# First additions held in their written order on VectorE, and a first norm in larger portions

## The chip, the cores and the metric

The kernel runs on one core of a Trainium2 chip. The metric is the device time of one execution in microseconds (us), as the median of several runs. A core has engines that run their own instruction streams side by side: TensorE (PE) does matmuls into PSUM, VectorE (DVE) and ScalarE (ACT) do element-wise work, GpSimd (POOL) helps in the first half, and SyncE (SP) issues the DMA transfers. Engines wait for each other through semaphores.

## The reference

Three blocks follow each other on 8 sequences of 576 tokens with 512 channels:

```python
# attention: 8 heads of 64, mask by blocks of 64 tokens
attn = softmax(where(block_i >= block_j, q @ k.T / 8, -1e9)) ; x = attn @ v
# gated mixer
gate = sigmoid(causal_conv(x, conv_w))            # 5 taps, by channel
x = (gate * (x @ w_val)) @ w_out
# Fourier mix, norm and feed-forward
u  = x + real(fft(fft(x, axis=1), axis=2))
un = (u - mean(u)) / sqrt(var(u) + 1e-6)
out = u + relu(un @ w_ch1) @ w_ch2                # 512 -> 2048 -> 512
```

## The kernel before

Products of fp32 numbers are made as three matmuls of high and low parts: every operand x is split into h (a cast on ScalarE) and x - h (a subtraction on VectorE).

The first 640 us are attention, mixer and transform; they write u, tokens along the free axis, to the tensor u_d. The rest is the norm and the feed-forward, and only that is touched.

**Straight products.** The first two blocks of 512 tokens (g = 0 and 1) go through the 16 blocks f of the weights with plain products: psh (lines 1489 to 1491), its relu split into HL (h on ScalarE, line 1493, low part on VectorE, line 1494), and the second product into o (1509 to 1511), one block behind. Beside them weights are loaded, decoded and summed (`combine`: four additions on VectorE at line 1203, a cast on ScalarE at 1227, low part at 1228, store to comb_d). In g = 1, from f = 6, the norm of the first pair of blocks is made beside them, by calls of `next(nxt)`, some steps at each f.

**Pairs.** The remaining tokens go in four pairs (blocks of 512, 512, 384 and 384 tokens) through products with seven in place of eight partial products. A pair has 56 steps n: in the first 28 (l = 0) four rounds i over the seven partial products in the order 1, 2, 6, 5, 7, 3, 4; in the last 28 (l = 1) seven over four i. A step is 12 matmuls into a pair of PSUM banks (`product`, lines 1414 to 1416). The banks are read out by a copy on ScalarE (1422) or an addition on VectorE (1427); 1424 is an addition of h to h, 1430 and 1432 are the relu. Partial product 6 of a round adds to the sums of partial product 1, two steps after it, and needs the copy of 1422 first. `prepare(k + LOOK)` makes an operand three steps ahead: ScalarE's cast at 1374, VectorE's low part at 1375, its source at 1319 (a difference of blocks). The operands lie in a ring of eight places, `ring_o = [10, 11, 12, 13, 8, 9, "HH", "U1"]`; the last one is also the source of the stores out<-U (line 1525) of the second straight block.

Three generators run beside the steps. `combine2` makes the other weight sums in units of a weight block: four additions on VectorE (`four`, line 1203), four casts packed<-two on ScalarE (1257), four low parts (1260), four stores to comb_d of 256 KB (1246). The packed buffers are two each of KP and KL, so the casts of one unit wait until the stores of the unit before have landed. `norm_x(g + 1)` makes the norm of the next pair, from X (loaded from u_d by `load_x` at n = 0): the sums u2 + u3 (line 1118, the first addition), u0 + u1 (1119) and their sum (1120), split into ah (1108, ScalarE) and al (1109, VectorE) for the mean on TensorE (1111, 1112); then X minus mean (1128), squares (1133), their sums (1135), root (1140), reciprocal (1141) and the scaling of X (1312). `load_chunk` loads weights; `load_y` loads u for the residual.

A scheduler orders the instructions of each engine by its own costs and the order in which the program traces them; `tc.keep_in_program_order(x)` ties an instruction behind all that was traced on its engine before it. SP's queue carries all transfers.

Of the kernel before, what the change touches and what calls it, by code (L numbers as in the profile page):

```python
# [9 lines left out]
F32R = mybir.dt.float32r  # L10
# [7 lines left out]
def kernel(  # L18
# [1030 lines left out]
    def phase2():  # L1049
        with ExitStack() as c2:  # L1050
# [61 lines left out]
                nc.tensor.matmul(ps, ones, l, start=False, stop=True)  # L1112
                yield

            def norm(u, n, done, hl=None, first=False):
                pool = nc.vector
                s1, s = (s2.tile([P, T], F32, tag="x", name=x)[:, 0:n] for x in ("s1", "s"))
                nc.vector.tensor_tensor(out=s1, in0=u[:, 2, :], in1=u[:, 3, :], op=ALU.add)
                pool.tensor_tensor(out=s, in0=u[:, 0, :], in1=u[:, 1, :], op=ALU.add)
                nc.vector.tensor_tensor(out=s, in0=s, in1=s1, op=ALU.add)  # L1120
                yield
                pm = ps_t.tile([P, T], F32, tag="t", name="pm")[:, 0:n]
                yield from average(pm, s, n, first)
                q = s5.tile([P, T], F32, tag="s", name="q")[:, 0:n]
                for t in range(4):
                    x = s2.tile([P, T], F32, tag="x", name="x")[:, 0:n]
                    c = x if hl else u[:, t, :]
                    nc.vector.tensor_tensor(out=c, in0=u[:, t, :], in1=pm, op=ALU.subtract)
                    if hl:
                        nc.scalar.copy(out=hl[0][:, t, :], in_=x)  # L1130
                        (pool if t % 2 else nc.vector).tensor_tensor(
                            out=hl[1][:, t, :], in0=x, in1=hl[0][:, t, :].bitcast(F32), op=ALU.subtract)
                    nc.scalar.activation(out=x if t else q, in_=c, func=AF.Square)
                    if t:
                        pool.tensor_tensor(out=q, in0=q, in1=x, op=ALU.add)
                    yield
                pv = ps_t.tile([P, T], F32, tag="t", name="pv")[:, 0:n]
                yield from average(pv, q, n, first)
                r = s5.tile([P, T], F32, tag="r", name="r")[:, 0:n]
                nc.scalar.activation(out=r, in_=pv, func=AF.Sqrt, bias=eps)  # L1140
                nc.vector.reciprocal(out=r, in_=r)
                yield
                yield from done(r)
# [43 lines left out]
            def load_w(f):  # L1187
# [9 lines left out]
                nc.scalar.copy(out=h, in_=x)  # L1197
                nc.vector.tensor_tensor(out=l, in0=x, in1=h.bitcast(F32), op=ALU.subtract)

            def four(t, a11, a12, a21, a22):  # L1200
                for z, a, b, op in ((0, a21, a22, ALU.add), (1, t[:, 0], a11, ALU.subtract),
                                    (2, a11, a21, ALU.subtract), (3, a12, t[:, 1], ALU.subtract)):
                    nc.vector.tensor_tensor(out=t[:, z], in0=a, in1=b, op=op)

            def combine():

# [27 lines left out]
            def combine2():  # L1234

                ins = {}

                def load(j):
                    if j < NH:
                        ins[j] = [kp.tile([P, S], F32, tag=t, name="ab")[:, 0:D] for t in ("K0", "K1")]  # L1240
                        for z in range(2):
                            nc.sync.dma_start(out=ins[j][z], in_=w_d[j + NH * z][:, D:2 * D])
                def keep(j, p):
                    z, jj = divmod(j, NH // 2)
                    for s in range(4):
                        nc.sync.dma_start(out=comb_d[1][z][s][:, jj * D:jj * D + D], in_=p[s].bitcast(F32))
                load(N2A)
                for j in range(N2A, NH):
                    load(j + 1)
                    yield  # L1250
                    x = [x.rearrange("p (y c) -> p y c", c=256) for x in ins.pop(j)]
                    t = s3.tile([P, 4, 256], F32, tag="st", name="two")
                    p = [kp.tile([P, S], F32R, tag=n, name="packed")[:, 0:D] for n in ("KP", "KL", "KP", "KL")]
                    four(t, x[0][:, 0], x[1][:, 0], x[0][:, 1], x[1][:, 1])
                    yield
                    for s in range(4):
                        nc.scalar.copy(out=p[s][:, 0:256], in_=t[:, s])
                    yield
                    for s in range(4):
                        nc.vector.tensor_tensor(out=p[s][:, 256:D], in0=t[:, s], in1=p[s][:, 0:256].bitcast(F32),  # L1260
                                                op=ALU.subtract)
                    yield
                    yield
                    keep(j, p)
# [41 lines left out]
            def norm_x(g):  # L1306
                if g >= NQ:
                    return
                for z in range(2):
                    def scale(r, u=X[g, z]):  # L1310
                        for t in range(4):
                            nc.vector.tensor_tensor(out=u[:, t, :], in0=u[:, t, :], in1=r, op=ALU.mult)
                            yield
                    yield from norm(X[g, z], NS[g], scale)

            T2 = {}

# [45 lines left out]
            def operand(k):  # L1363

                if k >= len(steps):
                    return
                g, l, p, i = steps[k]
                if l == 0 and i:
                    opnd[k] = opnd[k - 7]
                    return  # L1370
                x = source(k)
                o = at(ring_o[nitem[0] % len(ring_o)], [P, 2, 2, NS[g]], F32R, "o")
                nitem[0] += 1
                nc.scalar.copy(out=o[:, 0], in_=x)  # L1374
                nc.vector.tensor_tensor(out=o[:, 1], in0=x, in1=o[:, 0].bitcast(F32), op=ALU.subtract)  # L1375
                opnd[k] = o
# [84 lines left out]
            for g in range(NG):  # L1461
# [4 lines left out]
                for f in range(NF + 1):  # L1466
# [31 lines left out]
                        next(mix, None)  # L1498
                    if f > LG and late:
                        late.pop(0)()  # L1500
                    for _ in range(2 if g == 0 and f >= NL else 3 if g and f >= 6 else 1):
                        next(nxt, None)
                    if f == 0:
                        continue
# [30 lines left out]
            for k, (g, l, p, i) in enumerate(steps):  # L1535
                n = k % 56
                if n == 0:
                    load_x(g + 1)
                    nxt = norm_x(g + 1)
                if k % 2 == 0 and k:  # L1540
                    load_chunk(k // 2 + len(ring_w) - 1)
                if 24 <= n < 28:
                    load_y(g, (11, 12, 22, 21)[n - 24])
                prepare(k + LOOK)
                if n < 24:
                    next(mix, None)
                early(g, l, n - 28 * l)
                product(k)
                if n >= LP and late:
                    late.pop(0)()  # L1550
                if n >= 12:
                    next(nxt, None)

    phase1()
# [95 lines left out]
```

## Time and profile before

| what | us |
|---|---|
| median of 3 runs | 1416.41 |
| lowest and highest | 1414.26, 1420.87 |
| the profiled execution | 1415.93 |
| its span on the core | 1414.1 |
| TensorE busy in the span | 1353.9 (96%) |
| VectorE, ScalarE, GpSimd busy | 1097.1, 821.9, 207.8 |

A row of a timeline gives the start of an instruction from the span's start, how long it took, its engine and line, what it writes and reads (tile names without numbers), shape, and in square brackets how long the engine had been idle before it and what ended that. Equal neighbours are put into one row with a count. A matmul's record is longer than its share of TensorE, since matmuls are pipelined; the distance of two starts is what one costs. The granted clock (PEclk) is 1.00 or 0.50 of full speed.

### The profile page before, as it was taken

The page shows a single profiled execution, that of the slowest core. Times are in us where ns is not written, and L with a number is a line of the kernel's source. Part 1 is how long each engine was busy: PE and PEld are TensorE (multiplying, and loading weights), DVE is VectorE, ACT ScalarE, POOL GpSimd, SP SyncE. Part 2 cuts the span into 40 slices and gives each one's busy share as a digit, 9 for nine tenths or more (in the row PEclk, how much of TensorE's full clock was granted, in tenths as well). Part 3 has the DMA queues.
Part 4 walks back from the last instruction along what each step waited for, and adds up shares of the span by engine and source line. Part 5 has one row for each costly group of instructions (what it writes and reads, how often), then busy time and mean ns, then how long its engine had stood idle before and what let it go on. Part 6 is the DMA issues. An engine that isn't in the chain of part 4 may idle for free.

```text
span 1414.1 us, 24025 instructions
## 1 busy us (share of the span) xinstructions
PE 1353.9 (96%) x8547; PEld 1188.6 (84%) x8547; DVE 1097.1 (78%) x1965; ACT 821.9 (58%) x1790; POOL 207.8 (15%) x180
## 2 busy tenths in 40 slices
PE   5798999999999999999999998999999999999998
PEld 3576889898989898988787887788878889999998
DVE  5777697878878787989899798599637983796374
ACT  5677777687777777755344344564346533644451
POOL 3423232323232322321100000000000000000000
PEclk9799999999999999999999999999999999999999
DMA  7566666656565565546798976975875579779875
GB/s 211 147 174 191 154 177 162 179 140 182 142 176 153 159 159 147 168 141 226 249 331 317 369 281 213 322 237 197 283 254 201 179 244 321 251 251 323 271 249 188
DMA packets 176755, 308.24 MB, mean 218 GB/s; under 512 B 28270, under 2 KB 106876, under 8 KB 169468
## 3 DMA queue, kind: packets, MB, share of 16 engines
q1 hardware_dynamic: 176096, 306.57, 68.8%
q8 instruction: 68, 1.11, 0.3%
q14 instruction: 51, 0.42, 0.1%
q10 hardware_dynamic: 540, 0.14, 0.1%
HBM read 203.74 MB, written 56.76 MB: 184 GB/s over the span
## 4 chain that ended last, share of the span: by engine, by line
PE 70%; DVE 12%; DMA 7%; ACT 4%; issue 3%; POOL 2%; SPq 1%; DVEq 0%; ACTq 0%; POOLq 0%
PE banks L1414 11%; PE banks L1415 11%; PE banks L1416 11%; PE av L615 4%; PE pt L587 4%; PE sc L427 2%; DVE gate L642 2%; PE sc L428 2%; PE psh L1489 2%; PE psh L1491 2%; PE psh L1490 2%; PE o L1511 2%; PE o L1509 2%; PE o L1510 2%; PE psx L191 1%
## 5 line engine op out<-in xcount | busy, mean ns | idle before, releaser
L1414 PE MATMUL banks<-o,chunk 128*128 128x512 f32 (+1 forms) x896 | 326.3, 364 | 8.4 <-ACT h L1422 8.1
L1415 PE MATMUL banks<-o,chunk 128*128 128x512 f32 (+1 forms) x896 | 325.3, 363 | 0.0
L1416 PE MATMUL banks<-o,chunk 128*128 128x512 f32 (+1 forms) x896 | 325.3, 363 | 0.0
L473 ACT ACTIVATE PB<-sc,mx 128x128 f32<-128x128 f32 (+4 forms) x320 | 166.5, 525 | 51.5 <-DVE mx L459 27.8
L1414 PEld LDWEIGHTS banks<-o,chunk 128*128 128x128 f32 x896 | 168.9, 189 | 28.6 <-ACT h L1422 10.5
L1416 PEld LDWEIGHTS banks<-o,chunk 128*128 128x128 f32 x896 | 168.8, 188 | 17.8
L1415 PEld LDWEIGHTS banks<-o,chunk 128*128 128x128 f32 x896 | 169.0, 189 | 17.4
L1374 ACT CAST o<-h 128x1024 fp32r<-128x1024 f32 (+1 forms) x112 | 105.6, 945 | 112.2 <-PE banks L1416 93.9
L587 PE MATMUL pt<-ident,PB 128*128 128x128 f32 x800 | 141.4, 283 | 15.6 <-ACT PTb L593 8.1
L1375 DVE TENSOR_TENSOR o<-h,o 128x1024 fp32r<-128x1024 f32 (+1 forms) x112 | 119.7, 1088 | 28.0 <-ACT o L1374 20.9
L587 PEld LDWEIGHTS pt<-ident,PB 128*128 128x128 f32 x800 | 100.7, 144 | 32.3 <-ACT PTb L593 14.4
L642 DVE SCALAR_TENSOR_TENSOR gate<-XF,cw,gate 128x575 f32<-128x575 f32 (+3 forms) x128 | 122.5, 957 | 4.5 <-ACT gate L63 3.8
L459 DVE TENSOR_REDUCE mx<-sc 128x1 f32<-128x384 f32 (+2 forms) x192 | 104.3, 560 | 4.4 <-PE sc L193 2.7
L427 PE MATMUL sc<-K,QQ 128*128 128x256 f32 (+2 forms) x256 | 87.7, 353 | 12.9 <-DMA QQ<-QHL 12.0
L593 ACT COPY PTb<-pt 128x512 f32<-128x512 f32 (+1 forms) x160 | 86.5, 544 | 18.5 <-PE pt L587 17.8
L1422 ACT COPY h<-banks 128x1024 f32<-128x1024 f32 (+1 forms) x64 | 57.9, 906 | 53.0 <-PE banks L1416 52.8
L191 PE MATMUL psx<-GH,we_h 128*128 128x290 f32 x256 | 84.3, 329 | 2.4 <-ACT GH L57 1.5
L191 PE MATMUL psv<-XH,wv_h 128*128 128x288 f32 x256 | 83.4, 326 | 0.4 <-ACT PB L473 0.4
L428 PE MATMUL sc<-KL,QQ 128*128 128x256 f32 (+2 forms) x256 | 82.8, 334 | 0.0
L638 POOL TENSOR_TENSOR XL<-XF,XH 128x576 fp32r<-128x576 f32 x32 | 45.9, 1434 | 248.9 <-ACT XH L57 248.7
L1319 DVE TENSOR_TENSOR h<-h 128x1024 f32<-128x1024 f32 (+1 forms) x64 | 69.1, 1089 | 10.8 <-ACT h L1430 10.5
L192 PE MATMUL psx<-GL,we_h 128*128 128x290 f32 x256 | 76.9, 300 | 0.5 <-DVE GL L703 0.5
(266 smaller groups left out, 3162.9 us busy)
## 6 DMA issues: line engine op xcount, KB each, us to landing
chunk<-comb_d SPq DMA_DIRECT2D x64, 512.0 KB, 5.4
chunk<-comb_d SPq DMA_DIRECT2D x32, 1024.0 KB, 4.8
chunk<-base_d SPq DMA_DIRECT2D x48, 512.0 KB, 6.1
chunk<-base_d SPq DMA_DIRECT2D x24, 1024.0 KB, 5.7
K<-KP SPq DMA_DIRECT2D x128, 144.0 KB, 2.5
QQ<-QHL SPq DMA_DIRECT2D x128, 128.0 KB, 2.5
rw<-in_w_ch SPq DMA_DIRECT2D x28, 512.0 KB, 8.2
comb_d<-packed SPq DMA_DIRECT2D x12, 1024.0 KB, 9.3
```

The costliest lines, as they stand in the source:

```text
L191: nc.tensor.matmul(ps, lh, rh, start=first, stop=False)
L427: nc.tensor.matmul(t[:, o:o + w], q[:, 0, m], KK[p][h][:, 0:w], start=True, stop=False)
L428: nc.tensor.matmul(t[:, o:o + w], q[:, 1, m], KL[p][:, 0:w], start=False, stop=True)
L459: nc.vector.reduce_max(out=mx[:, j:j + 1], in_=t, axis=AX.X, negate=one)
L473: nc.scalar.activation(out=PB[i][:, k0:k0 + w], in_=t, func=AF.Exp, bias=nm, accum_out=su[:, at + j:at + j + 1])
L587: nc.tensor.transpose(ps[:, j, :], PB[i][:, (j0 + j) * P:(j0 + j + 1) * P], ident)
L642: nc.vector.scalar_tensor_tensor(out=gate[c][:, s:S], in0=XF[:, 0:S - s], scalar=cw[:, c, 4 - s:5 - s], in1=gate[c][:, s:S], op0=ALU.mult, ...
L1374: nc.scalar.copy(out=o[:, 0], in_=x)
L1375: nc.vector.tensor_tensor(out=o[:, 1], in0=x, in1=o[:, 0].bitcast(F32), op=ALU.subtract)
L1414: nc.tensor.matmul(to, wh, o[:, 0, x], start=first, stop=False, skip_group_check=not begin)
L1415: nc.tensor.matmul(to, wh, o[:, 1, x], start=False, stop=False, skip_group_check=not begin)
L1416: nc.tensor.matmul(to, wl, o[:, 0, x], start=False, stop=last, skip_group_check=not begin)
```

## The change

Five edits. (1) `norm` takes a flag `pin`: for the norms of the pairs after the first pair of blocks (g > 0), the first addition u2 + u3 is tied behind all that was traced on VectorE before it. (2) `four` does so with the first of its four additions, once `combine2` has begun. (3) The eighth operand of the ring (item 7) and all later ones count from place 0 of the ring again, so item 7 takes place 10, not U1. (4) In g = 1 from f = 6 on, the norm of the first pair is advanced by four steps at each f, before by three. (5) In the pair loop `combine2` is advanced at the steps 4 to 27, before at 0 to 23, and the next pair's norm from step 10, before from 12.

```diff
-            def norm(u, n, done, hl=None, first=False):
+            def norm(u, n, done, hl=None, first=False, pin=False):
...
-                nc.vector.tensor_tensor(out=s1, in0=u[:, 2, :], in1=u[:, 3, :], op=ALU.add)
+                add = nc.vector.tensor_tensor(out=s1, in0=u[:, 2, :], in1=u[:, 3, :], op=ALU.add)
+                if pin:
+                    tc.keep_in_program_order(add)
...
+            pin = [False]
+
             def four(t, a11, a12, a21, a22):
...
-                    nc.vector.tensor_tensor(out=t[:, z], in0=a, in1=b, op=op)
+                    made = nc.vector.tensor_tensor(out=t[:, z], in0=a, in1=b, op=op)
+                    if pin[0] and z == 0:
+                        tc.keep_in_program_order(made)
...
                     x = [x.rearrange("p (y c) -> p y c", c=256) for x in ins.pop(j)]
+                    pin[0] = True
...
-                    yield from norm(X[g, z], NS[g], scale)
+                    yield from norm(X[g, z], NS[g], scale, pin=g > 0)
...
-                o = at(ring_o[nitem[0] % len(ring_o)], [P, 2, 2, NS[g]], F32R, "o")
+                o = at(ring_o[nitem[0] if nitem[0] < 7 else (nitem[0] - 7) % len(ring_o)], [P, 2, 2, NS[g]], F32R, "o")
...
-                    for _ in range(2 if g == 0 and f >= NL else 3 if g and f >= 6 else 1):
+                    for _ in range(2 if g == 0 and f >= NL else 4 if g and f >= 6 else 1):
...
-                if n < 24:
+                if 4 <= n < 28:
                     next(mix, None)
...
-                if n >= 12:
+                if n >= 10:
                     next(nxt, None)
```

Each engine has as many instructions after as before; their order differs from the first pair's norm on. Seven lines come in ahead of the second half, so that lines move: 1118 stays, 1203 becomes 1207, 1257 becomes 1264, 1319, 1374, 1375, 1422, 1427 and 1494 become 1326, 1381, 1382, 1429, 1434 and 1501.

On VectorE, at the end of the second straight block, before (X_10248 and X_10245 are the first pair's two blocks, two and ab belong to the weight sums):

```order
L1494 SCALAR_TENSOR_TENSOR HL<-psh,HL 128x512
L1203 TENSOR_TENSOR two<-ab 128x256
L1109 TENSOR_TENSOR al<-q,ah 128x512
L1203 TENSOR_TENSOR two<-two,ab 128x256
L1203 TENSOR_TENSOR two<-ab,two 128x256
L1141 RECIPROCAL r<-r 128x512
L1228 TENSOR_TENSOR packed<-two,packed 128x4x256
L1312 TENSOR_TENSOR X_10248<-X_10248,r 128x512
L1494 SCALAR_TENSOR_TENSOR HL<-psh,HL 128x512
L1312 TENSOR_TENSOR X_10248<-X_10248,r 128x512 x3
L1494 SCALAR_TENSOR_TENSOR HL<-psh,HL 128x512
```

and after:

```order
L1143 RECIPROCAL r<-r 128x512
L1207 TENSOR_TENSOR two<-ab 128x256
L1319 TENSOR_TENSOR X_10248<-X_10248,r 128x512
L1207 TENSOR_TENSOR two<-two,ab 128x256
L1207 TENSOR_TENSOR two<-ab 128x256
L1207 TENSOR_TENSOR two<-ab,two 128x256
L1319 TENSOR_TENSOR X_10248<-X_10248,r 128x512 x3
L1234 TENSOR_TENSOR packed<-two,packed 128x4x256
L1501 SCALAR_TENSOR_TENSOR HL<-psh,HL 128x512 x2
```

The reciprocal has moved ahead of the low part that stood before it, and two low parts now follow each other behind the scaling.

On VectorE, some ten rows on, at the last operands of the first round, before:

```order
L1319 TENSOR_TENSOR X_10245<-T_10746,X_10245 128x1024
L1203 TENSOR_TENSOR two<-ab 128x256 x2
L1203 TENSOR_TENSOR two<-two,ab 128x256
L1319 TENSOR_TENSOR X_10245<-X_10245,T_10746 128x1024
L1375 TENSOR_TENSOR o<-X_10245,o 128x1024
```

and after:

```order
L1326 TENSOR_TENSOR X_10245<-T_10746,X_10245 128x1024
L1326 TENSOR_TENSOR X_10245<-X_10245,T_10746 128x1024
L1207 TENSOR_TENSOR two<-ab 128x256
L1382 TENSOR_TENSOR o<-X_10245,o 128x1024 x2
```

The two subtractions now follow each other, and one addition of the weight sums is left beside the operands.

On ScalarE, in the first two rounds of the first pair (banks_10768 to banks_10770 are the three pairs of PSUM banks), before:

```order
L1374 CAST o<-X_10245 128x1024
L1257 CAST packed<-two 128x256 x3
L1374 CAST o<-X_10245 128x1024
L1422 COPY h<-banks_10768 128x1024
L1257 CAST packed<-two 128x256
```

and after, there and some ten rows on:

```order
L1381 CAST o<-X_10245 128x1024 x2
L1429 COPY h<-banks_10768 128x1024
L1437 ACTIVATE h<-h 128x1024
...
L1429 COPY h<-banks_10769 128x1024
L1264 CAST packed<-two 128x256 x2
L1108 CAST ah<-s 128x512
L1264 CAST packed<-two 128x256
L1437 ACTIVATE h<-h 128x1024
L1429 COPY h<-banks_10769 128x1024
```

The packed casts have left the place ahead of the first round's copy and stand between two copies of the second round.

## Rows read from the trace of the kernel before

**Rows 1.** The page, part 1: busy time, share of the span and instructions.

```profile
PE 1353.9 (96%) x8547; PEld 1188.6 (84%) x8547; DVE 1097.1 (78%) x1965; ACT 821.9 (58%) x1790; POOL 207.8 (15%) x180
```

**Rows 2.** TensorE's waits, 850 to 1414 us: total, times, longest, in us.

```profile
PE banks L1414 <- ACT h L1422: 8.1, 5, 3.5
PE banks L1414 <- DVE o L1521: 0.3, 1, 0.3
```

**Rows 3.** Windows: length, busy of PE, PEld, DVE, ACT, POOL, PEclk, DMA, GB/s.

```profile
863.00:869.80 6.80, 5.56 (x13) 4.41 (x14) 6.80 (x15) 2.59 (x5) 0.00 (x0) 0.50 0.72 217
...
950.00:1000.00 50.00, 50.00 (x222) 41.43 (x221) 49.46 (x52) 20.14 (x21) 0.00 (x0) 1.00 0.60 209
```

**Rows 4.** Timeline of TensorE: the last matmul before the long wait, and the waits.

```profile
860.33 0.39 PE L1416 MATMUL banks<-o,chunk 128*128 128x512 f32 x1
864.24 0.80 PE L1414 MATMUL banks<-o,chunk 128*128 128x512 f32 x1 [3.52 <-ACT h L1422]
...
896.02 0.51 PE L1414 MATMUL banks<-o,chunk 128*128 128x512 f32 x1 [1.44 <-ACT h L1422]
...
913.70 0.50 PE L1414 MATMUL banks<-o,chunk 128*128 128x512 f32 x1 [0.54 <-ACT h L1422]
...
1030.89 0.50 PE L1414 MATMUL banks<-o,chunk 128*128 128x512 f32 x1 [1.22 <-ACT h L1422]
...
1187.92 0.45 PE L1414 MATMUL banks<-o,chunk 128*128 128x384 f32 x1 [1.37 <-ACT h L1422]
```

**Rows 5.** Timeline of ScalarE, 860 to 864 us.

```profile
860.01 1.05 ACT L1374 CAST o<-X 128x1024 fp32r<-128x1024 f32 x1 [4.75 <-DVE X L1319]
860.96 1.01 ACT L1257 CAST packed<-two 128x256 fp32r<-128x256 f32 x3
862.23 1.04 ACT L1374 CAST o<-X 128x1024 fp32r<-128x1024 f32 x1 [0.25 <-DVE X L1319]
863.18 1.00 ACT L1422 COPY h<-banks 128x1024 f32<-128x1024 f32 x1
```

**Rows 6.** Timeline of VectorE, the same stretch.

```profile
859.88 0.76 DVE L1203 TENSOR_TENSOR two<-ab 128x256 f32<-128x256 f32 x2
860.56 0.42 DVE L1203 TENSOR_TENSOR two<-two,ab 128x256 f32<-128x256 f32 x1
860.89 1.23 DVE L1319 TENSOR_TENSOR X<-X,T 128x1024 f32<-128x1024 f32 x1
```

**Rows 7.** Timeline of VectorE, about the first pair's reciprocal.

```profile
839.63 0.69 DVE L1494 SCALAR_TENSOR_TENSOR HL<-psh,HL 128x512 fp32r<-128x512 f32 x1
...
842.74 3.35 DVE L1141 RECIPROCAL r<-r 128x512 f32<-128x512 f32 x1 [0.69 <-ACT r L1140]
```

**Rows 8.** Timeline of ScalarE, the operand cast before the wait at 896.

```profile
893.41 1.05 ACT L1374 CAST o<-h 128x1024 fp32r<-128x1024 f32 x1 [3.21 <-DMA chunk<-comb_d]
```

**Rows 9.** SP's queue, the last store of the second straight block.

```profile
884.63 0.40 SPq L1525 DMA_DIRECT2D out<-U  x1
```

**Rows 10.** Timeline of ScalarE, before the wait at 913.

```profile
910.90 0.88 ACT L1257 CAST packed<-two 128x256 fp32r<-128x256 f32 x2 [0.85 <-DMA comb_d<-packed]
```

**Rows 11.** Stores of a unit of weight sums on SP, ScalarE's casts behind them.

```profile
873.96 1.42 SPq L1246 DMA_DIRECT2D comb_d<-packed  x3
...
880.65 0.41 ACT L1257 CAST packed<-two 128x256 fp32r<-128x256 f32 x1 [0.38 <-DMA comb_d<-packed]
881.90 0.41 ACT L1257 CAST packed<-two 128x256 fp32r<-128x256 f32 x1 [0.84 <-DMA comb_d<-packed]
```

**Rows 12.** DMA issues: out<-in, queue, count, KB each, median us from issue to landing.

```profile
chunk<-comb_d SPq DMA_DIRECT2D x64, 512.0 KB, 5.4
...
comb_d<-packed SPq DMA_DIRECT2D x16, 256.0 KB, 7.6
```

**Rows 13.** Timeline of VectorE, the first additions of two later norms.

```profile
1026.27 0.56 DVE L1118 TENSOR_TENSOR s<-X 128x384 f32<-128x384 f32 x1 [6.15 <-DMA X<-u_d]
...
1184.26 0.56 DVE L1118 TENSOR_TENSOR s<-X 128x384 f32<-128x384 f32 x1 [4.97 <-DMA X<-u_d]
```

## The prediction, made before the changed kernel ran

> **What bounds the kernel now.** I read the page first: TensorE has a matmul running for 96% of the span [rows 1], so time can go only where it stands still or runs at its lower clock. Both kernels hold the same instructions and the order on the engines is the same up to about 803 us, so I asked for TensorE's waits from 850 us on, where the paired products begin. The reader is to see two entries: five waits of 8.1 us in all for line 1422, ScalarE's copy of a bank out of PSUM, and one of 0.3 us [rows 2]. Elsewhere TensorE is full: from 950 to 1000 us it is busy for 50.00 of 50 us with 222 matmuls [rows 3], that is one every 0.225 us, and VectorE beside it is busy for 49.46 us.
>
> A wait costs more than its idle time. A matmul's record lasts 0.39 us while the next begins after 0.225, so 0.16 us of the gap is already inside the record, and the first one behind a wait takes 0.50 us in place of 0.39 [rows 4]: together some 0.27 us on top. The five waits are then 1.44 + 0.27 = 1.7, 0.54 + 0.27 = 0.8, 1.22 + 0.27 = 1.5, 1.37 + 0.27 = 1.6 us, and the long one at 864.24. This one idles for 3.52 us and ends 864.24 - 860.33 - 0.225 = 3.7 us late. Behind it the granted clock is 0.50, which is 1.2 GHz, from 863.00 to 869.80 [rows 3]: 13 matmuls are busy for 5.56 us there, and at the full rate 13 take 2.9, so 2.6 us are lost besides. All five with the lower clock hold 11.9 us; no more can be had there.
>
> **The change part by part.** The sum is made against the profiled run, 1415.93 us with a span of 1414.1.
>
> *Late at the first pair (864.24).* The copy at 863.18 stands on ScalarE behind a cast of line 1374 that waited for VectorE [rows 5], and between them lie three packed casts of line 1257. VectorE had put three first-half additions of the later weight sums (line 1203, 859.88 to 860.97) ahead of the operand's subtraction at 860.89 [rows 6], and ran without a break. In the changed order the subtraction stands ahead of all but one of them and the packed casts have left ScalarE's row. On the other side, the larger portions bring the norm's reciprocal, 3.35 us, ahead of two low parts of line 1494, of which one was made at 839.63, before it [rows 7]. Walking VectorE's new row with the durations of the old one, TensorE misses that low part for about 1.65 us in the last straight products (between nothing and the reciprocal's 3.35), the operands of the first pair are done at 860.0 in place of 862.1, and the copy lets the product start at about 862.15 in place of 864.24: -2.1 us. The 1.65 us are not added, since the product that waited needs the copy, not TensorE's arrival; they use up the idle time that stood there. What is left of a wait there is some 0.2 us. Behind the waits of 1.22 to 1.44 us the first matmul takes 0.50 or 0.51 us, behind the long one 0.80 [rows 4]: the short ones brought no lower clock, so I take it as gone: -2.6 us. Moved with the norm are its two TensorE matmuls per sum, earlier by about two weight blocks and of the same number: nothing.
>
> *The operand ring (896.02).* ScalarE's cast of line 1374 at 893.41 idled for 3.21 us [rows 8]. The trace names a chunk load; the place it writes, U1, is also read by the store out<-U issued at 884.63 [rows 9], and 893.41 lies 8.8 us behind it, while that chunk has nothing to do with the place. Two bank copies stood behind it. In the new ring the cast takes place 10, and ScalarE's new order has it later, where no copy is due: -1.7. Every later operand moves on by one place; its last reader is then seven operands back, with 3 us or more of lead by my walk, at no cost. Without that lead each late operand would cost a step of 2.7 us.
>
> *Later weight sums four steps on.* A step is 12 matmuls, 12 x 0.225 = 2.7 us, so 16 stores, their 16 x 0.25 MB and the loads of ab leave SP's queue some 11 us later, and pass chunk and y loads on SP. This takes the wait at 913.70 away, where packed casts waited 0.85 us for a store [rows 10]: -0.8. It also makes a **new wait**. A unit's casts need the buffers that the unit before is still storing: in the kernel before, stores issued from 873.96 on let casts go at 880.65 and 881.90 [rows 11], 6.7 to 8.0 us later. In the new order the first unit's stores leave at about 875.5 to 876.3, and two packed casts of the second unit stand right behind the first copy of the second round, at which ScalarE arrives at 879.6. They wait until 882.2 to 884.3. Queued behind them on ScalarE are the norm's first cast, one more packed cast, a relu that wants a VectorE addition, and the bank copy that TensorE needs at 886.65 (862.15 and nine steps). By the walk that copy ends between 886.4 and 889.3, so this wait costs 0 to 2.9 us with the 0.27; I take 1.7, nearer to the upper landing since the median store takes 7.6 us [rows 12]: +1.7. The units after it have about 0.5 us in hand. The last chunk made of these sums stands behind the y loads on SP, and by a landing of 5.4 us [rows 12] still has some 5 us.
>
> The Trainium skill ("DMA: Bandwidth & Descriptors", section "Anatomy of one DMA — SWDGE (gpsimd) path") fits a DMA as about 2.0 us plus bytes over 436 GB/s, which would be an estimate of 2.6 us for such a store, and there would then be no new wait at all: the 1.7 us would drop out of the sum. The fit is for transfers that GpSimd issues, these are SP's, and the trace disagrees with it for them (6.7 us at the least).
>
> *First additions of the pairs' norms (1030.89, 1187.92).* VectorE sat on line 1118 for 6.15 and 4.97 us until the load of X landed [rows 13], with the addition or subtraction behind it that feeds ScalarE and so the copy. In the new order the addition stands behind the readouts of its step: -1.5 and -1.6. What is late next there is nothing on TensorE: the norm is used some 25 steps on. The start of the norm two steps earlier (n >= 10) can give back at most what these two removed, if the load is still not there.
>
> Sum: -2.1 - 2.6 - 1.7 - 0.8 - 1.5 - 1.6 + 1.7 = -8.6, so 1415.93 - 8.6 = 1407.3. The median of the runs before, 1416.41, is 0.5 above the profiled run, so on that scale **1407.8 us**. Faster or slower is called from 0.5% on (7.1 us, about what can be told from no change): faster means below 1409.3.
>
> **The rivals.** *No new wait:* stores land in 6 us or less. For it: two of the 16 need only be a little quicker. Against it: [rows 11, 12]. The sum is -10.3: 1406.1. *A long new wait:* the second unit's casts wait for the slower landing (2.9 us in place of 1.7) and TensorE falls to 1.2 GHz behind it as it did at 864.24, 2.6 more. That is -10.3 + 5.5 = -4.8: 1411.6. *The gain at the first pair does not come:* the missed low part costs the whole 3.35 us, the products start as late as before and the clock falls all the same. Left are -1.7 - 0.8 - 3.1 + 1.7 = -3.9: 1412.5. *Slower:* the stores of the later sums, now issued beside the round's chunk loads and out<-U stores, land after 11.5 us. ScalarE is then held for 5.8 us with the bank copy behind it and the lower clock after it (5.8 + 2.6), and the last chunk, behind the y loads, is 3.5 us late with the same (3.5 + 2.6): -10.3 + 14.5 = +4.2, 1420.6. It decides from landings above 11 us; the median of 7.6 speaks against it. *The change does not do what it says* (the tied additions stand where they stood): the orders shown above exclude it on VectorE.
>
> **How the numbers follow.** The forecast 0.42, no new wait 0.18, a long one 0.20, no gain at the first pair 0.12, slower 0.08. Faster holds "no new wait" and about 0.37 of the forecast (its upper end, 2.9 us of new wait, is 1409.0, and the runs spread): 0.55. The two long cases and the rest of the forecast are the same: 0.37. Slower: 0.08. The range goes down to all five waits gone, 1416.41 - 11.9 = 1404.5, and up beyond 1412.5 by half a microsecond: 1404.5 to 1413.0; the slower case and a part of the two long ones stay outside.
>
> **What would show it.** Right: no wait of over 0.5 us on the first pair's third product and a granted clock of 1.00 from 860 to 870; nothing near 1030 and 1187; a wait of 1 to 3 us of TensorE for the bank copy in the pair's second round, with ScalarE's packed cast idle for a store ahead of it. Wrong: a stall above 2 us in the last straight products, a stretch of 0.50 clock, a cast of an operand waiting for its ring place, or a new wait for a chunk at the end of the first pair.

## The result, and the profile after

The changed kernel takes 1406.13 us (median of 6 runs, 1404.02 to 1407.26), the kernel before 1417.37 (median of 6, 1414.26 to 1420.87): ratio 0.9919, 95% interval 0.9901 to 0.9937. The forecast was 1407.8 in a range of 1404.5 to 1413.0, and faster. The profiled runs are nearer to each other than the medians: 1415.93 before, low among its runs, and 1406.78 after, from the upper half of its own.

The page of the changed kernel answers [rows 1] with a span 9.1 us shorter:

```profile
span 1405.0 us, 24014 instructions
...
PE 1349.6 (96%) x8547; PEld 1186.2 (84%) x8547; DVE 1094.1 (78%) x1965; ACT 821.1 (58%) x1790; POOL 207.7 (15%) x180
```

Its TensorE waits from 840 us on, total, times and longest (before: [rows 2]): the five waits for the bank copy of line 1422, now 1429, have become one, and a wait for HL is new.

```profile
PE o L1518 <- DVE HL L1501: 1.7, 1, 1.7
PE banks L1421 <- ACT h L1429: 1.0, 1, 1.0
```

The two profiled runs already differ by some 0.6 us when the part with the change begins. For the comparisons I therefore take a stretch that both have: from the matmul that waits for the first decoded weights, just past 703 us, to the last matmul. Of the kernel before, TensorE's timeline has

```profile
703.13 0.50 PE L1489 MATMUL psh<-UTH,W 128*128 128x512 f32 x1 [1.09 <-ACT W L1197]
...
1409.76 0.34 PE L1416 MATMUL banks<-o,chunk 128*128 128x384 f32 x1
```

and of the changed one

```profile
703.76 0.50 PE L1496 MATMUL psh<-UTH,W 128*128 128x512 f32 x1 [1.02 <-ACT W L1199]
...
1400.60 0.34 PE L1423 MATMUL banks<-o,chunk 128*128 128x384 f32 x1
```

That is 706.63 and 696.84 us: 9.8 us less. I call it the **late stretch** below; it leaves out what goes on before 703.

At the start of the first pair, VectorE's timeline has the reciprocal 4 us earlier than in [rows 7], two low parts behind the scaling in one row, and the second subtraction at 859.09, not 860.89 [rows 6]:

```profile
838.72 3.35 DVE L1143 RECIPROCAL r<-r 128x512 f32<-128x512 f32 x1
...
846.96 1.28 DVE L1501 SCALAR_TENSOR_TENSOR HL<-psh,HL 128x512 fp32r<-128x512 f32 x2
...
859.09 1.22 DVE L1326 TENSOR_TENSOR X<-X,T 128x1024 f32<-128x1024 f32 x1
```

ScalarE's casts and the bank copy follow it, with no packed cast between them (before: [rows 5]):

```profile
860.42 1.06 ACT L1381 CAST o<-X 128x1024 fp32r<-128x1024 f32 x1 [0.16 <-DVE X L1326]
861.38 1.00 ACT L1429 COPY h<-banks 128x1024 f32<-128x1024 f32 x1
```

TensorE's timeline has the three places of which the prediction spoke, the wait for HL, the third product of the pair, and the new wait in the second round (before: [rows 4]):

```profile
847.70 1.21 PE L1518 MATMUL o<-HL,W 128*128 128x512 f32 x4 [1.67 <-DVE HL L1501]
...
862.43 0.50 PE L1421 MATMUL banks<-o,chunk 128*128 128x512 f32 x1
...
888.20 0.50 PE L1421 MATMUL banks<-o,chunk 128*128 128x512 f32 x1 [1.00 <-ACT h L1429]
```

The third product starts 0.28 us behind the matmul ahead of it (862.15), against 3.9 before, and the window from 863 on, with the columns of [rows 3], is at the full clock of 2.4 GHz:

```profile
863.00:870.00 7.00, 7.00 (x32) 5.81 (x31) 3.45 (x5) 2.97 (x3) 0.00 (x0) 1.00 0.87 281
```

The new wait is read on ScalarE and on SP. The casts behind the copy at 879.08 idle for a store. The relu behind them waits for an addition of VectorE (884.94 to 886.16), which stands behind the low parts of those casts, and the copy that TensorE needs ends at 888.15:

```profile
879.08 1.02 ACT L1429 COPY h<-banks 128x1024 f32<-128x1024 f32 x1 [1.43 <-PE banks L1423]
882.48 0.41 ACT L1264 CAST packed<-two 128x256 fp32r<-128x256 f32 x1 [2.38 <-DMA comb_d<-packed]
883.37 0.41 ACT L1264 CAST packed<-two 128x256 fp32r<-128x256 f32 x1 [0.48 <-DVE packed L1267]
...
886.19 1.06 ACT L1437 ACTIVATE h<-h 128x1024 f32<-128x1024 f32 x1 [1.59 <-DVE h L1434]
887.16 0.99 ACT L1429 COPY h<-banks 128x1024 f32<-128x1024 f32 x1
```

```profile
876.03 1.40 SPq L1252 DMA_DIRECT2D comb_d<-packed  x3
...
879.97 0.48 SPq L1252 DMA_DIRECT2D comb_d<-packed  x1
```

The store was issued at 876.03 and the cast began at 882.48, 6.4 us later; the median landing of these stores is now 8.1 us (7.6 in [rows 12]):

```profile
comb_d<-packed SPq DMA_DIRECT2D x16, 256.0 KB, 8.1
```

### The profile page after: what moved, and what is told of

The parts are those of the page before. It is cut to its first block, busy times and chain, and to the rows that moved or that the text cites. A ratio compares the mean times of both kernels' runs of the same rounds, so it can differ in the third digit from the quotient of the medians.

```text
span 1405.0 us, 24014 instructions
## 1 busy us (share of the span) xinstructions
PE 1349.6 (96%) x8547; PEld 1186.2 (84%) x8547; DVE 1094.1 (78%) x1965; ACT 821.1 (58%) x1790; POOL 207.7 (15%) x180
## 4 chain that ended last, share of the span: by engine, by line
PE 73%; DVE 12%; DMA 5%; ACT 3%; issue 3%; POOL 2%; SPq 2%; DVEq 0%; ACTq 0%; POOLq 0%
PE banks L1421 12%; PE banks L1423 12%; PE banks L1422 12%; PE av L615 4%; PE pt L587 4%; DVE gate L642 2%; PE sc L427 2%; PE o L1518 2%; PE psh L1498 2%; PE psh L1496 2%; PE psh L1497 2%; PE o L1516 2%; PE o L1517 2%; PE sc L428 2%; POOL XA L848 1%
## 5 line engine op out<-in xcount | busy, mean ns | idle before, releaser
L192 PE MATMUL psv<-XL,wv_h 128*128 128x288 f32 x256 | 76.2, 298 | 0.0
```

The costliest lines, as they stand in the source:

```text
L192: nc.tensor.matmul(ps, lh, rl, start=False, stop=False)
```

## The experiments

A line of the change is undone or done alone in most of them. Measured are TensorE's waits and the late stretch of the profiled run, and the median where it says more. The spread of the medians (the kernel before: 1417.4 to 1419.4 in the four sets of runs) is larger than most single terms, so that the terms rest on the trace, and that is one execution of each kernel. One row of the table needs a warning: from its first matmul to a wait near 771 that all kernels have, e6 takes 69.47 us, the others 67.95 to 68.10. Its clock was low for 3.4 us there, so that 1.4 us of its late stretch have nothing to do with its edit.

| kernel | first matmul at 703, last matmul | late stretch | median, ratio to before, interval |
|---|---|---|---|
| before | 703.13, 1409.76 | 706.6 | |
| changed | 703.76, 1400.60 | 696.8 | 1406.13, 0.9919 (0.9901 to 0.9937) |
| e1, no tie on the weight sums | 703.22, 1401.20 | 698.0 | 1407.56, 0.9927 (0.9908 to 0.9946) |
| e2, small portions | 701.64, 1400.39 | 698.7 | 1406.74, 0.9925 (0.9905 to 0.9945) |
| e3, old ring | 703.75, 1400.81 | 697.1 | 1406.10, 0.9912 (0.9894 to 0.9931) |
| e4, no tie on the norms | 702.81, 1406.52 | 703.7 | 1409.32, 0.9942 (0.9922 to 0.9962) |
| e5, portions alone | 702.80, 1404.49 | 701.7 | 1412.77, 0.9943 (0.9920 to 0.9967) |
| e6, ring alone | 701.91, 1408.49 | 706.6 | 1416.51, 0.9987 (0.9973 to 1.0001) |
| e7, additions on GpSimd | 703.99, 1403.24 | 699.3 | 1407.78, 0.9914 (0.9897 to 0.9932) |
| e8, the same, early stores | 706.14, 1405.27 | 699.1 | 1409.83, 0.9931 (0.9914 to 0.9947) |
| e9, portions and norm tie | 702.83, 1401.42 | 698.6 | 1409.00, 0.9929 (0.9901 to 0.9957) |
| e10, old steps of the weight sums | 702.68, 1399.37 | 696.7 | 1405.94, 0.9904 (0.9875 to 0.9933) |
| e11, norm from step 12 | 705.02, 1403.95 | 698.9 | 1407.44, 0.9921 (0.9898 to 0.9944) |
| e12, early stores | 703.44, 1400.37 | 696.9 | 1406.51, 0.9910 (0.9883 to 0.9938) |

**What removed the long wait at 864.** Three kernels tell it apart: the tie, the portions, and the portions alone.

```diff
e1
-                    pin[0] = True
+                    pin[0] = False
e2
-                    for _ in range(2 if g == 0 and f >= NL else 4 if g and f >= 6 else 1):
+                    for _ in range(2 if g == 0 and f >= NL else 3 if g and f >= 6 else 1):
```

> The changed kernel without the tie on the first addition of the later weight sums. On VectorE the two subtractions of the first pair's operands still stand ahead of all but one of these additions, on ScalarE the first unit's four packed casts move up to right behind the first round's copy. Theory A (each edit removes the wait that the walk gave it, and the long wait at 864 went through the order of the operands, not through this tie): TensorE's third product of the pair still starts without a wait of over 0.5 us and at full clock; the first unit's stores leave some 10 us earlier, so the casts of the second unit no longer wait for them and the 1.0 us wait of TensorE at 888 shrinks to under 0.3: 1.3 us less than the changed kernel, 1404.8 on its median 1406.1. Theory B (the tie is what keeps VectorE free at the start of the pair): the wait at 862 comes back with 2 us or more and the lower clock behind it, 1408 to 1411.

> The changed kernel with the first pair's norm in portions of three as before. Its reciprocal is back behind the low part, so theory A expects no wait of TensorE for HL near 847 (1.67 us in the changed kernel), but VectorE's second subtraction of the first pair ends about 1 us later than in the changed kernel, only about 1 us ahead of where it was before, and the third product of the pair then waits 2.4 us in place of 3.5 before and 0.1 now. If the clock stays up behind a wait of that length, the sum is about 0.9 us more than the changed kernel (1407.0); if it falls as behind the 3.5 us, 3.5 us more (1409.6). Theory B (the portions do nothing for the operands, only the order does): the wait at 862 is under 1 us and the time 1 to 2 us below the changed kernel.

Without the tie (e1) the third product started as in the changed kernel: theory A as to the long wait. Its second half failed, the wait at 888 stayed at 0.78 us and one of 0.97 came at 908 (e12 below has the reason). With the small portions (e2) the wait is back, 2.51 us where 2.4 was expected, and the clock fell behind it; TensorE's row and the windows about it, with the columns of [rows 3]:

```profile
861.63 0.79 PE L1421 MATMUL banks<-o,chunk 128*128 128x512 f32 x1 [2.51 <-ACT h L1429]
...
860.00:863.00 3.00, 1.37 (x3) 1.16 (x4) 3.00 (x4) 1.58 (x2) 0.00 (x0) 0.69 0.02 5
863.00:870.00 7.00, 7.00 (x29) 5.67 (x28) 2.66 (x4) 2.98 (x3) 0.00 (x0) 0.89 0.91 211
```

So the order of the subtractions, with which e2 still goes, takes 1.0 us off the 3.5, and with the portions the rest goes too. The clock was low for 3.4 us there (0.31 x 3 / 0.5 + 0.11 x 7 / 0.5), not 6.8, and the wait at 888 was only 0.2; the late stretch is 1.9 us longer than that of the changed kernel.

```diff
e5 (on the kernel before)
-                    for _ in range(2 if g == 0 and f >= NL else 3 if g and f >= 6 else 1):
+                    for _ in range(2 if g == 0 and f >= NL else 4 if g and f >= 6 else 1):
```

> The kernel before with the larger portions alone (four steps of the first pair's norm at each weight block; no ties, old ring, old step bounds). Theory A' (the long wait at 864 is set by how much VectorE still has to do when the pair begins; the portions bring the reciprocal forward and with that do most of it): the order now has the bank copy behind one operand cast and three packed casts, so the third product starts at about 862.2, the point to which the new 1.67 us wait for HL near 847 has moved TensorE: no wait there above 0.5 us, no lower clock. Gain 3.7 + 2.6 - 1.9 = 4.4 us on the kernel before; the waits at 896, 1030 and 1187 stay. Theory B' (the additions of the weight sums ahead of the operands, which the ties and the later start take away, set it): a wait of 1 us or more is left at 862 and the gain is under 3 us.

The portions alone took the long wait and the low clock (1.00 from 860 to 870) away altogether, though three additions of the weight sums (858.20 to 859.29) still stood ahead of the second subtraction at 859.21. That speaks for theory A' as to the edit, but not for VectorE's work alone: ScalarE's order changed as well, and the bank copy now stands ahead of the cast of the operand that this subtraction makes:

```profile
859.27 1.01 ACT L1264 CAST packed<-two 128x256 fp32r<-128x256 f32 x3
860.19 1.01 ACT L1429 COPY h<-banks 128x1024 f32<-128x1024 f32 x1
861.10 1.05 ACT L1381 CAST o<-X 128x1024 fp32r<-128x1024 f32 x1
```

Counted from the matmul near 703, that copy ends at 161.05 us in the kernel before, 159.95 in e2, 158.62 in the changed kernel and 158.40 in e5. TensorE was due at the third product at about 157.4 without the larger portions and at about 158.6 with them, since it had waited for HL. So they close the gap from both sides: the copy comes earlier, and TensorE comes 1.2 us later. How much of the copy's gain in e5 is VectorE's earlier work and how much ScalarE's order, no run separates; an estimate from the rows is that with the cast ahead the copy would end near 862.4 in place of 861.2, and TensorE, due at 861.45, would wait about 1 us. TensorE's waits from 840 us on are 1.67 us for HL, 0.36 and 0.25 in the first pair, and 2.72 and 1.60 at the starts of the third and fourth pair:

```profile
PE banks L1421 <- ACT h L1429: 4.9, 4, 2.7
PE o L1518 <- DVE HL L1501: 1.7, 1, 1.7
```

The late stretch fell by 4.9 us (4.4 expected).

**The norms' tie.**

```diff
e4
-                    yield from norm(X[g, z], NS[g], scale, pin=g > 0)
+                    yield from norm(X[g, z], NS[g], scale)
```

> The changed kernel without the tie on the norms' first addition. On VectorE line 1118 stands ahead of a bank readout again at the start of the third and the fourth pair. Theory A: VectorE sits there until X has landed, 4 to 6 us, and TensorE waits for the bank copy near 1020 and 1177, idle 1.2 and 1.4 us as before: 3.1 us more than the changed kernel, 1409.2. Theory B (the earlier start of the norm or the shorter pair before it has already moved the load far enough): idle under 0.3 us at both places, 1406.1 to 1406.6.

Theory A, and by more than expected: 3.90 us of idle time at 1026, 1.21 at 1185, and 6.9 us in the late stretch. VectorE's row has the cause, the untied addition ahead of the readouts, behind 8.83 us of waiting for X (6.15 in [rows 13]); TensorE's row follows:

```profile
1021.67 0.56 DVE L1118 TENSOR_TENSOR s<-X 128x384 f32<-128x384 f32 x1 [8.83 <-DMA X<-u_d]
```

```profile
1026.29 0.79 PE L1421 MATMUL banks<-o,chunk 128*128 128x512 f32 x1 [3.90 <-ACT h L1429]
```

Counted from the matmul near 703, the product that waits there was due 7.0 us earlier than in the kernel before, X landed 4.3 us earlier: the wait grew by the 2.7 us between them. Whatever makes the first pair faster brings TensorE sooner to a load that doesn't come sooner by as much; e5 shows the same (2.72 us in place of 1.22). The clock then fell for 3.4 us, some 1.6 us more.

**The ring.**

```diff
e3
-                o = at(ring_o[nitem[0] if nitem[0] < 7 else (nitem[0] - 7) % len(ring_o)], ...)
+                o = at(ring_o[nitem[0] % len(ring_o)], ...)
e6 (on the kernel before)
-                o = at(ring_o[nitem[0] % len(ring_o)], ...)
+                o = at(ring_o[nitem[0] if nitem[0] < 7 else (nitem[0] - 7) % len(ring_o)], ...)
```

> The changed kernel with the old ring, so the eighth operand takes place U1 again. ScalarE's order has its cast behind the copy of the second round again, ahead of another bank copy. Theory A: the cast idles until the last store out<-U has landed, 8 to 9 us behind its issue (at 882.4 in the changed kernel, so until about 891), and TensorE waits once for the bank copy behind it, idle 1 to 2 us near 891 to 896: 1.3 to 2.3 us more than the changed kernel, 1407.4 to 1408.4. Theory B (the old wait at 896 was for the chunk load that the trace named, or went with the shift of the weight sums): no such wait, 1406.1.

> The kernel before with the new ring alone. The changed kernel with the old ring had no wait for U1, since its last out<-U store left 2 us earlier and the cast came after it had landed. Theory A: in the kernel before the same cast does wait for that store, so with the ring alone the wait of 1.44 us at 896 goes: 1.7 us less. Theory B: the wait at 896 was for something else (a chunk load, as the trace names it): it stays, and the time is that of the kernel before. The long wait at 864 and those at 1030 and 1187 stay in both.

In e3 the cast to U1 stood behind the copy again and did not idle at all:

```profile
888.58 1.01 ACT L1429 COPY h<-banks 128x1024 f32<-128x1024 f32 x1
889.49 1.05 ACT L1381 CAST o<-h 128x1024 fp32r<-128x1024 f32 x1
```

In e6 the cast was gone from that place, and ScalarE idled until the same time (893.41 in [rows 8]), for the packed casts that stand behind it:

```profile
893.44 0.92 ACT L1264 CAST packed<-two 128x256 fp32r<-128x256 f32 x2 [3.12 <-DMA comb_d<-packed]
```

So two waits ended together in the kernel before: the operand's cast on its place, and the packed casts behind it on a store of the weight sums. Taking one away left the other. That the cast does wait for its place is named in e5, and with 2.82 us in e9, which have the old ring and the old steps too; TensorE waited only 0.36 and 0.45 us behind it there, so that most of the wait at 896 goes with the portions. The row is e5's:

```profile
887.30 1.05 ACT L1381 CAST o<-h 128x1024 fp32r<-128x1024 f32 x1 [2.74 <-DMA out<-U]
```

In e6 the wait at 896 fell from 1.44 to 0.62 us, and those at 878 and 913 rose to 0.88 and 1.12. At 878 the packed cast ahead of the bank copy went at the same time, in the kernel before and in e6, waiting for its store:

```profile
876.07 0.41 ACT L1257 CAST packed<-two 128x256 fp32r<-128x256 f32 x1 [2.43 <-DMA comb_d<-packed]
876.18 0.41 ACT L1264 CAST packed<-two 128x256 fp32r<-128x256 f32 x1 [3.38 <-DMA comb_d<-packed]
```

TensorE was there 0.7 us earlier, since the clock behind 864 was low for 3.4 us and not for 6.8. At 913 the copy began at 912.51, before at 912.65. What TensorE gained ahead of these stores, it lost at them. That the late stretch came out the same is chance in part: the 1.4 us at its start stand against the shorter low clock behind 864 and shorter waits at 1030 and 1187 (0.98 and 0.51 us). The rows show no gain by the ring; the median (0.9987, 0.9973 to 1.0001) leaves both open, no gain and the 1.7 us of the forecast.

**The two edits that are left.**

```diff
e9 (on the kernel before)
+                if pin:
+                    tc.keep_in_program_order(add)
...
-                    yield from norm(X[g, z], NS[g], scale)
+                    yield from norm(X[g, z], NS[g], scale, pin=g > 0)
...
-                    for _ in range(2 if g == 0 and f >= NL else 3 if g and f >= 6 else 1):
+                    for _ in range(2 if g == 0 and f >= NL else 4 if g and f >= 6 else 1):
```

> The kernel before with two of the edits, the larger portions and the tie of the norms' first addition; no tie on the weight sums, old ring, old step bounds. Theory A'' (these two carry the whole change, the other three bring 1 us or less together): TensorE waits 1.67 us for HL near 847, under 0.6 us each near 889 and 907 as with the portions alone, and not at all at 1025 and 1183: from the start of the weight blocks near 703 to the end 701.5 us, the changed kernel's 701.2 give or take 0.5 (the kernel before: 711.0). Theory B'' (the step bounds or the tie on the weight sums are needed with them): a wait of over 1 us in the first pair, 703 or more.

It carries 8.0 of the 9.8 us: 698.6, against 701.5 expected from a stretch that I had measured to the end of the span, which is 4.3 to 4.4 us longer (so 697.1 on this scale). A wait of TensorE for the norm's al, 0.68 us, and one of 0.45 for the bank copy make up for most of the difference:

```profile
PE o L1518 <- DVE HL L1501: 1.7, 1, 1.7
PE pm L1112 <- DVE al L1109: 0.7, 1, 0.7
PE banks L1421 <- ACT h L1429: 0.4, 1, 0.4
```

Theory A'' holds for the bulk and misses 1.8 us.

```diff
e10
-                if 4 <= n < 28:
+                if n < 24:
                     next(mix, None)
e11
-                if n >= 10:
+                if n >= 12:
                     next(nxt, None)
```

> The changed kernel with the later weight sums advanced at steps 0 to 23 again. Of their additions one stands between the last two subtractions of the first pair's operands on VectorE, 0.34 us. Theory A'': the third product waits 0.3 to 0.6 us, the wait at 888 goes down to 0.3 to 0.8 since the first unit's stores leave earlier, and a wait of 1 us may show one round later as without the tie: 0 to 1 us more than the changed kernel from 703 to the end (701.2 to 702.2). Theory B'' (the later start is what frees the first pair): a wait of 1 us or more at 862 with the lower clock behind it, 704 or more.

> The changed kernel with the next pair's norm started at step 12 as before. The tie keeps the first addition behind the readouts in any case, so theory A'' expects nothing at the pairs' starts; the norm's first cast leaves ScalarE's crowded place in the second round, so the wait at 888 falls by up to its 0.5 us: 700.7 to 701.2 from 703 to the end. Theory B'' (the two steps are needed for the norm to be ready for the next pair): a new wait of TensorE for an operand near the end of a pair, 702 or more.

The later start of the weight sums (e10) is worth nothing here: the wait at 888 is gone, the third product waits 0.27 us, and the late stretch is 0.1 us shorter than the changed kernel's (all its waits from 840 us on):

```profile
PE o L1518 <- DVE HL L1501: 1.7, 1, 1.7
PE banks L1421 <- ACT h L1429: 0.3, 1, 0.3
```

The two steps of the norm (e11) are worth 2.1 us, against my expectation: the wait at 888 stayed (0.91) and one of 0.61 came at 929; besides, the norm's two matmuls then stand within steps, and at eight places the matmul beside them begins 0.06 to 0.15 us late, 0.9 us together. Neither is the wait for an operand that theory B'' named.

**The new wait, and two attempts to beat the change.**

```diff
e12 (and e8, with the additions of e7)
-                    pin[0] = True
+                    pin[0] = False
...
-                    yield
-                    yield
                     keep(j, p)
+                    yield
+                    yield
e7
-                    four(t, x[:, 0, 0], a12, a21, x[:, 1, 1])
+                    four(t, x[:, 0, 0], a12, a21, x[:, 1, 1], nc.gpsimd if k >= 9 else nc.vector)
```

> The changed kernel with the twelve additions of the last three units of the first weight sums (line 1207 inside combine) on GpSimd, which is idle there; VectorE has 12 x 0.34 = 4.1 us less to do before the first pair. Theory A' (VectorE's work up to the first pair's operands is the limit, and the 1.67 us wait for HL is where it shows): the low part stands ahead of the reciprocal again, the wait near 847 goes, no wait comes back at 862, and the whole 1.67 + 0.27 = 1.9 us is gained: 1404.2. Theory B' (GpSimd's additions are slow or slow VectorE down, or the pair start is held by ScalarE or a load): the wait only moves to 862, gain under 0.5 us.

> As the run before (GpSimd additions), and besides without the tie on the later weight sums and with each unit's four stores issued right after its low parts are made, in place of two steps later. Without the tie alone the first unit's stores were ready at 866.5 but left SP only at 874 to 880, behind chunk loads that wait for TensorE, and TensorE waited 0.8 and 1.0 us at 888 and 908. If SP's order was what held them, they leave at about 867 to 875 now, land before ScalarE comes to the next unit's casts, and both waits shrink to under 0.3 us: 1.9 + 1.3 us less than the changed kernel, 1402.9. If the landing itself is what counts, the wait at 888 stays and the time is 1404.2 to 1405.

> The changed kernel without the tie on the weight sums and with each unit's four stores issued right behind its low parts, no GpSimd additions. If the wait at 888 is set by how early the first unit's stores leave SP, it falls to under 0.3 us as in the run with GpSimd (0.15), the one at 908 to about 0.7, the 1.67 us for HL stay: 1 us less than without the tie alone, 701.4 from 703 to the end. If it was GpSimd's relief of VectorE that took it away there, it stays at 0.8 and the time is 702.4.

In e1 the first unit's low parts were ready at 866.5, and three of its stores left SP at 874.07, behind a chunk load that waits for TensorE:

```profile
865.08 1.44 DVE L1267 TENSOR_TENSOR packed<-two,packed 128x256 fp32r<-128x256 f32 x4
```

```profile
874.07 2.34 SPq L1252 DMA_DIRECT2D comb_d<-packed  x3
```

With the stores traced right behind the low parts (e12) two of them left at 869.68, and the waits at 888 and 908 went (0.09 and 0.14 us are left at 882 and 907, too small for the list). It was SP's order that held them, and the landing that then set the wait; GpSimd had no part in it.

```profile
869.68 0.80 SPq L1252 DMA_DIRECT2D comb_d<-packed  x2
```

```profile
PE o L1518 <- DVE HL L1501: 1.7, 1, 1.7
```

The late stretch is 1.0 us shorter than e1's and the same as the changed kernel's. Moving twelve additions to GpSimd (e7) removed the wait for HL and cost more than that: the record of one addition is 0.73 to 1.60 us there, in place of 0.41 on VectorE, and the norm came later, with new waits of TensorE in the straight products and 1.0 us at the third product of the pair. VectorE lost time as well: beside the two additions of 1.6 us its low part of the packed weights took 1.75 us (1.22 at 848.94), and the al at 841.80 took 1.22 (0.69 in the changed kernel at 884.33). That is theory B'.

```profile
837.61 1.51 POOL L1207 TENSOR_TENSOR two<-ab 128x256 f32<-128x256 f32 x2 [5.60 <-DMA ab<-w_d]
839.20 1.60 POOL L1207 TENSOR_TENSOR two<-two,ab 128x256 f32<-128x256 f32 x1
840.88 1.59 POOL L1207 TENSOR_TENSOR two<-ab,two 128x256 f32<-128x256 f32 x1
...
840.13 1.75 DVE L1234 TENSOR_TENSOR packed<-two,packed 128x1024 fp32r<-128x1024 f32 x1
```

```profile
PE banks L1421 <- ACT h L1429: 2.0, 2, 1.0
PE pm L1111 <- ACT ah L1108: 1.2, 1, 1.2
PE pv L1112 <- DVE al L1109: 0.7, 1, 0.7
```

e8 has much the same waits, but for the one in the second round, which is 0.15, and one of 0.67 at 912. No kernel beats the changed one by more than the runs spread; e10 and e12 are level with it. The two together, and a lighter VectorE between 834 and 862 us by other means, were not tried.

## Why the prediction was right, and where it wasn't

That the sum came near is luck in part: the order of the additions and the ring were credited with what the portions do. By its own steps, on the late stretch (9.8 us less; the sum said 8.6); a wait's restart is the 0.27 us that the prediction adds to it:

- **The first pair's start**, -2.1 and -2.6: right in size. Before, the wait, its first slow matmul and the low clock cost 6.4 us; after, the wait for HL with its restart costs 1.94 and the third product 0.16. That is -4.3, where the sum had -4.7; some 0.9 us of it belong to this execution, since behind the same wait of 3.52 us in e6 the low clock was half as long and TensorE was back 0.85 us sooner. The 1.67 us for HL came out as walked (1.65), and did use up idle time. What was wrong is whose merit it is: I gave it to the order of the additions and treated the larger portions as its price. e5 shows that the portions are enough, alone in part by another order on ScalarE; e1 and e10 show that neither the tie on the weight sums nor their later start is needed, e2 that the order alone takes 1.0 of the 3.5 us.
- **The operand ring**, -1.7: the step that failed. The wait did go, but not through the ring (e3: 0.2 us without it; e6: no gain in its rows; e5: 0.36 us left with the old ring). That the operand's cast waits for the store out<-U was right (e5 and e9 name it). But behind it stood packed casts whose own store landed at the same time, and I didn't look at what they waited for.
- **The weight sums four steps on**, -0.8 and +1.7: the new wait came where it was said, behind the packed casts, 1.0 us of idle time and 1.27 in all. Its price is the shift's own: without the shift (e10) it isn't there, and the wait at 913 isn't either. So the edit is worth nothing beside the others, where the two terms together made it a loss of 0.9.
- **The norms' first additions**, -1.5 and -1.6: both waits are gone. In the company of the other edits the tie is worth 6.9 us (e4), since the wait that it prevents grows with the speed of what comes before, and in e4 the clock fell behind it.
- **Not in the sum:** the 0.28 us wait at 857.70 with its restart, 0.55 us, and 0.2 at 878 went as well; the two steps of the norm, which I took for nothing, are worth 2.1 (e11).

The terms that the trace has, -4.3 - 0.55 - 0.2 - 1.7 - 0.8 - 1.5 - 1.6 + 1.27, add up to -9.4 of the 9.8. "No new wait" and "a long new wait" were the two sides of the forecast; 1.27 lies between them, and the clock didn't fall behind it. The Trainium skill's fit ("DMA: Bandwidth & Descriptors", section "Anatomy of one DMA — SWDGE (gpsimd) path"), made for transfers that GpSimd issues, gives an estimate of 2.6 us for such a store and would have left no wait; the measured 6.4 us from issue to the cast decide against using it for these SP stores.

## What to carry to other kernels

When two engines' waits end at the same time, the row names one of them: before a term is booked for an edit, ask what the next instruction in the queue waits for, since removing one wait may only uncover the other. Here the stall at the start of a stage was relieved by finishing the work ahead of it earlier, the norm under the straight products, more than by reordering what was left; and a speed-up upstream makes a load or store downstream that doesn't move with it later by as much (e4, e5, e6), so that an instruction that waits for one has to stand behind those that others wait for. The undoing of one edit at a time prices it in company, the edit alone prices it by itself, and the two differ (the portions 1.9 and 4.9 us): do both before naming what carries a change.

## What was not expected of the hardware

- The granted clock after a wait of TensorE did not follow the wait's length alone. Waits of 2.51, 3.52 and 3.90 us (e2, e6, e4) were followed by 3.4 us at 0.50, one of 3.52 in the kernel before by 6.8 us, one of 2.72 us (e5) by none, and so were all of 1.67 us or less from 840 us on; but one of 1.24 us at 702 (e6) had 3.4 us of it behind it, and the same wait in the other runs, 1.02 to 1.57 us, had none. The 2.6 us that the sum took for it is the cost in one execution; in e4 it was about 1.6.
- A 256-wide fp32 addition took 0.73 to 1.60 us on GpSimd and 0.41 on VectorE, and beside the slowest two a subtraction on VectorE took 1.75 us in place of 1.22 (e7).
